# Threshold attention, then a gated MLP: the mask of chunk 0 of six early pairs moved from GpSimd to ScalarE (five) and VectorE (one)

## The chip, the cores and the metric

The kernel runs on one core of a Trainium2 chip. A core has a matrix engine (TensorE, PE in the profile), a vector engine (VectorE, DVE), an engine for functions of one value (ScalarE, ACT), a general engine (GpSimd, POOL), and SyncE (SP), which here only issues DMAs. They run side by side, each through its own list of instructions in order, and wait for one another with semaphores. The metric is the time of one execution on the device in microseconds (us), lower is better.

## The reference

The inputs are q, k and v of shape (8, 8, 576, 64): batch, heads, sequence, head size. All is float32.

```python
scores = scale * np.matmul(q, k.transpose(0, 1, 3, 2))          # scale = 1/8
thresh = np.max(scores, axis=-1, keepdims=True) - tau           # tau = 0.02
scores = np.where(scores >= thresh, scores, -1000000000.0)
scores = scores - np.max(scores, axis=-1, keepdims=True)
attn = np.exp(scores)
attn = attn / (np.sum(attn, axis=-1, keepdims=True) + 1e-09)
x = np.matmul(attn, v)                    # heads side by side: (8, 576, 512)

h = np.maximum(x @ w_in, 0.0)             # (8, 576, 1024)
u, v = h[..., :512], h[..., 512:]
v_n = (v - mean(v)) / np.sqrt(var(v) + 1e-06)
v_s = einsum('ts,bsd->btd', w_spatial, v_n) + b_spatial[None, :, None]
return (u * v_s) @ w_out                  # (8, 576, 512)
```

In the softmax, a score more than tau below the maximum of its row counts as zero. What is kept of a row before the division is called its numerators here. The division is done after the product with v, by a row sum that comes out of that product as a further column.

## The kernel before

**Pairs, chunks, steps.** Two heads form a pair; there are 32 pairs, four to a batch. The 576 queries of a pair are cut into chunks 0 to 3 of 128 and a rest of 64. The rests of an even pair and the next odd one are taken together as chunk 4 at the start of the odd pair. The list `steps` thus has 144 entries (i, c): four for an even pair, in the order 0, 1, 2, 3, and five for an odd one, in the order 4, 0, 1, 2, 3. Step numbers 0 to 3 are pair 0, 4 to 8 pair 1, 9 to 12 pair 2, 13 to 17 pair 3, and so on; pair 7 begins with step 31.

**One step.** `step(i, c, fs)` (line 599) writes out the order of every engine by hand:

- TensorE forms the scores of the chunk for both heads in a PSUM tile `s` (lines 562 and 567). There are two such tiles, so that the scores of a step are made while those of the step before are being read.
- Up to two small jobs of the list `fs` follow on TensorE, with their evictions: the transposes of the next pair's q and k (line 246), products with v (290, 295), and, from step 26 on, the matmuls of the gated MLP, one job a step.
- VectorE takes the negated maximum of each row, `negm` (line 611).
- ScalarE reads `s` twice, once per head, and writes `e` (float32, 128 x 1152, three buffers).

**The mask**, in three forms. For chunks 2 and 4 (`on_act`, line 571) VectorE first adds tau to the negated maximum (line 615). ScalarE then applies Prelu with a slope of 1e30 (line 628): where score - maximum + tau is negative, the result is hugely negative, elsewhere it is unchanged. A further Exp (line 630) turns that into the bf16 numerators, with zeros where the score was under the threshold; exp(tau) cancels in the division. For the other chunks ScalarE applies Exp directly (line 634), and one step later `mask()` (line 575) compares `e` with `ctau` = exp(-tau) and multiplies. For chunks 1 and 3, and for chunk 0 of pairs 0 and 7 to 31, that is one instruction of VectorE (line 592). For chunk 0 of pairs 1 to 6 it is two of GpSimd, which write a bf16 tile `keep` of ones and zeros (line 587) and then the product (line 589).

The numerators lie in `p` (four tiles, each with two chunks). After chunk 1 and after chunk 3, `mask()` has SyncE issue a DMA that transposes the whole tile to `pT` (line 596). For chunk 4 the numerators lie in `pr`. They are transposed on TensorE for the first six pairs (the three entries of `r_on_pe`), with an eviction at line 394, and by DMA after that. This is so before and after the change.

**What else the queues hold.** SyncE issues all loads of q, k and v for two pairs at a time, one DMA a step, into a ring of two slots, and these DMAs stand in one queue with the transposes. GpSimd, in order, copies the loaded q and k into the order that the transposes need (line 137, at chunk 2), casts v to bf16 (157, 161, at chunk 0), copies a small piece of k into `kd` (269), which the next pair's scores need, casts the weights in the first 55 steps (174, 203, 206, 182), and from step 26 on does the small arithmetic of the normalisation (453 to 465). ScalarE also evicts the transposes (251, 253, 264), those of x (375) and of `pr` (394), and the MLP's products (445, 459, 492, 541). VectorE also does the division (302, 304) and the gating (521, 524).

Of the kernel before, what the change touches and what calls it, by code (L numbers as in the profile page):

```python
# [9 lines left out]
BF16 = mybir.dt.bfloat16  # L10
AX = mybir.AxisListType
ALU = mybir.AluOpType
# [5 lines left out]
def kernel(  # L18
# [17 lines left out]
    nc = tc.nc  # L36
# [6 lines left out]
    P = 128  # L43
    const = ctx.enter_context(tc.tile_pool(name="const", bufs=1))
# [19 lines left out]
    ctau = const.tile([P, 1], F32, name="ctau")  # L64
# [25 lines left out]
        for t in vn_ring:  # L90
            nc.vector.memset(t[64:128, 4, :], 1.0)

    keep = const.tile([P, 1152], BF16, name="keep")
    w_in = const.tile([P, 4, 1024], BF16, name="w_in")
    w_o = const.tile([P, 4, 512], BF16, name="w_o")
    wsT = const.tile([P, 5, 640], BF16, name="wsT")
# [455 lines left out]
    def scores(i, c):  # L552

        s = ps_s.tile([P, 1536], F32, name="s")
        if c < 4:
            who = [(i, slice(c * P, (c + 1) * P), slice(0, P))]
        else:
            who = [(i - 1 + k, slice(512, 576), slice(64 * k, 64 * k + 64)) for k in range(2)]  # L560
        for n, m, rows in who:
            nc.tensor.matmul(out=view(s[rows], 512, [[448, 2], [1, 64]]), lhsT=qks[n][:, 0, m],  # L562
                             rhs=kd_ring[n % 2], start=True, stop=True)
        for h in range(2):
            hs = slice(64 * h, 64 * h + 64)
            for n, m, rows in who:
                nc.tensor.matmul(out=s[rows, 1024 * h:1024 * h + 512], lhsT=qks[n][hs, 0, m],  # L567
                                 rhs=qks[n][hs, 1, 0:512], start=True, stop=True)
        return view(s, 0, [[960, 2], [1, S]])

    def on_act(c):

        return c in (2, 4)

    def mask():
        i, c, e = unmasked.pop()
        if c == 4:
            dst = pts[i // 2] = ptr_ring[i // 2 % 2]
            if i // 2 in r_on_pe:
                return  # L580
            nc.sync.dma_start_transpose(out=dst, in_=pr_ring[i // 2 % 2])
            return
        pt = p_ring[2 * (i % 2) + c // 2]
        if c == 0 and 0 < i < 7:

            ef = e.rearrange("p h s -> p (h s)")
            nc.gpsimd.tensor_scalar(out=keep, in0=ef, scalar1=ctau, scalar2=1.0,  # L587
                                    op0=ALU.is_ge, op1=ALU.mult)
            nc.gpsimd.tensor_tensor(out=pt[:, c % 2, :], in0=ef, in1=keep, op=ALU.mult)  # L589
        elif not on_act(c):  # L590
            ef = e.rearrange("p h s -> p (h s)")
            nc.vector.scalar_tensor_tensor(out=pt[:, c % 2, :], in0=ef, scalar=ctau, in1=ef,  # L592
                                           op0=ALU.is_ge, op1=ALU.mult)
        if c % 2:
            dst = pts[i, c // 2] = ptp.tile([P, 2, 9, P], BF16, name="pT")
            nc.sync.dma_start_transpose(out=dst.rearrange("p c b s -> p (c b) s"),
                                        in_=pt.rearrange("p c s -> p (c s)"))

    def step(i, c, fs):

        s = scores(i, c)
        while held:
            held.pop(0)()


        for kind, mm, ev in fs[:2]:
            mm()
            if kind == "act":
                ev()
        nm = small.tile([P, 2], F32, name="negm")  # L610
        nc.vector.tensor_reduce(out=nm, in_=s, axis=AX.X, op=ALU.max, negate=True)  # L611

        by = scale if c == 4 else 1.0
        if on_act(c):
            nc.vector.tensor_scalar(out=nm, in0=nm, scalar1=by, scalar2=float(tau),  # L615
                                    op0=ALU.mult, op1=ALU.add)
        for kind, mm, ev in fs[:2]:
            if kind == "dve":
                ev()
        due = [f for n, f in later if n <= 0]  # L620
        later[:] = [(n - 1, f) for n, f in later if n > 0]
        for f in due:
            f()
        e = ep.tile([P, 2, S], F32, name="e")
        if on_act(c):

            for h in range(2):
                nc.scalar.activation(out=e[:, h, :], in_=s[:, h, :], func=ACT.Prelu,  # L628
                                     bias=nm[:, h:h + 1], scale=by, alpha=1e30)
            nc.scalar.activation(out=pr_ring[i // 2 % 2] if c == 4 else p_ring[2 * (i % 2) + c // 2][:, c % 2],  # L630
                                 in_=e.rearrange("p h s -> p (h s)"), func=ACT.Exp)
        else:
            for h in range(2):
                nc.scalar.activation(out=e[:, h, :], in_=s[:, h, :], func=ACT.Exp,  # L634
                                     bias=nm[:, h:h + 1])
        ready = sends[:]
        sends.clear()
        if unmasked:
            mask()
        for f in ready:  # L640
            f()
        unmasked.append((i, c, e))
        for kind, mm, ev in fs[2:]:
            mm()
            if kind == "dve":
                ev()
            else:
                held.append(ev)
# [150 lines left out]
    with tc.manual_schedule():  # L799
# [23 lines left out]
        for g, (i, c) in enumerate(steps):  # L823
            if c == 2 and i + 2 < NPAIR:
                shape_qk(i + 2)
            if c == 0:
                shape_v(i)
            if c == 0 and i % 2 and i + 3 < NPAIR or g == 0:
                for w in range(3):
                    queue.extend(load(i + (3 if g else 2), 2, w))  # L830
            if g in chores:
                chores[g][0](chores[g][1])
            fs, small_ones = [], []
            if i + 1 < NPAIR and c < 3:
                fs.append(qk_rem(i + 1) if c == 1 else qk_main(i + 1, c // 2))
            if i and c == (2 if i % 2 else 3):
                fs.append(pv(i - 1, 0))
            if i > 1 and c == 4:
                fs.append(pv(i - 2, 1))
            if i % 2 and c == 3:  # L840
                fs.append(pv(i - 1, 1))
            if i % 2 and i > 1 and c == 1:
                small_ones = [pv_rest(i // 2 - 1)]
                fs += small_ones
            fs += [f(*a) for f, *a in jobs.get(g, [])]
            fs.sort(key=lambda f: (f[0] == "dve", f in small_ones))
            sends += queue[:1 if g > 3 else 2]
            del queue[:1 if g > 3 else 2]
            step(i, c, fs)
# [8 lines left out]
        while held:  # L858
            held.pop(0)()
        mask()  # L860
        inner.close()
        wide.append(ctx.enter_context(tc.tile_pool(name="ps_t", bufs=6, space=PSUM,
# [49 lines left out]
```

## Time and profile before

| | us |
|---|---|
| median of 3 runs (lowest to highest) | 501.4 (501.18 to 501.8) |
| profiled execution, its own time | 501.18 |
| its span, first to last instruction | 499.4 |
| TensorE busy | 457.5 |
| VectorE busy | 420.2 |
| ScalarE busy | 385.5 |
| GpSimd busy | 263.1 |
| `keep`, line 587: 6 instructions, each | 4.176 |
| GpSimd's product, line 589: 6 instructions, mean | 2.752 |
| VectorE's mask, line 592: 90 instructions, mean | 1.481 |
| ScalarE's further Exp, line 630 to `p`: 32 instructions, mean | 1.163 |
| bias plus tau on VectorE, line 615: 48 instructions, mean | 0.453 |

A line of the trace gives the start and the duration in us, the engine, the line of the kernel (L587 is line 587), the operation and the tiles, written as output<-input. In brackets stands the time that the engine was idle before the instruction, and what ended that idle time. PE is the matmul, PEld the loading of its weights. Times in the text are from the start of the span. In the slices of the page one slice is 12.5 us and a digit is the busy share in tenths; PEclk is the clock that TensorE was granted, in tenths of its full clock.

### The profile page before, as it was taken

To read this page: it belongs to the slowest core of one execution; us is meant where nothing else is said; L and a number is where in the kernel's file an instruction comes from. 1 tells how busy PE (TensorE), PEld (TensorE's weight loads), DVE (VectorE), ACT (ScalarE), POOL (GpSimd) and SP (SyncE) were. 2 spreads that over 40 slices of the span, in tenths; PEclk is the share of its full clock that TensorE was granted. 3 is DMA by queue.
4 is the path that set the end of the run, shared out by engine and by line. 5 is a ranking of instruction groups with operands and counts; after the bars stand their busy time and mean duration, and the time that the engine had idled before them with its cause. 6 is when DMAs were issued, how large, how long until landed. Compare 5 with 4: busy or idle time off the path is not lost.

```text
span 499.4 us, 9898 instructions
## 1 busy us (share of the span) xinstructions
PE 457.5 (92%) x3646; PEld 243.9 (49%) x3691; DVE 420.2 (84%) x557; ACT 385.5 (77%) x672; POOL 263.1 (53%) x415
## 2 busy tenths in 40 slices
PE   7768787859989999999999999999999999999995
PEld 4334443435455455545454555545455555545542
DVE  5897898866988998799988998899898998899573
ACT  4847667767897979788887989787987889797351
POOL 3597585998462764357433753366424744253021
PEclk9887988997999999999999999999999999999998
DMA  7947868768698989997899989999999989867523
GB/s 241 235 95 178 190 138 193 162 145 165 146 178 211 194 178 220 200 205 167 176 199 216 177 198 210 198 184 180 180 203 218 178 182 214 158 108 131 145 82 109
DMA packets 227568, 88.49 MB, mean 177 GB/s; under 512 B 197056, under 2 KB 221760, under 8 KB 227520
## 3 DMA queue, kind: packets, MB, share of 16 engines
q1 hardware_dynamic: 226864, 86.98, 83.3%
q8 instruction: 29, 0.48, 0.4%
q0 software_dynamic: 160, 0.52, 0.3%
q10 hardware_dynamic: 496, 0.36, 0.2%
q14 instruction: 19, 0.16, 0.1%
HBM read 33.31 MB, written 9.44 MB: 86 GB/s over the span
## 4 chain that ended last, share of the span: by engine, by line
PE 52%; ACT 19%; DVE 16%; issue 5%; POOL 4%; DMA 2%; SPq 0%; POOLq 0%; ACTq 0%; DVEq 0%
PE s L567 16%; DVE negm L611 7%; ACT e L634 6%; PE s L562 5%; DVE p L592 5%; PE f L246 5%; PE f L295 4%; ACT e L628 4%; PE f L536 4%; PE f L477 3%; DVE negm L615 3%; PE f L507 2%; PE f L435 2%; PE f L290 2%; POOL keep L587 2%
## 5 line engine op out<-in xcount | busy, mean ns | idle before, releaser
L611 DVE TENSOR_REDUCE negm<-s 128x2 f32<-128x1152 f32 x144 | 194.8, 1353 | 40.5 <-PE s L567 40.0
L567 PE MATMUL s<-qkT 64*128 64x512 f32 (+1 forms) x640 | 168.1, 659 | 0.0
L634 ACT ACTIVATE e<-s,negm 128x576 f32<-128x576 f32 x192 | 131.7, 741 | 14.7 <-POOL p L589 5.0
L592 DVE SCALAR_TENSOR_TENSOR p<-e,ctau 128x1152 bf16<-128x1152 f32 x90 | 133.3, 1481 | 4.3 <-ACT e L634 4.2
L562 PE MATMUL s<-kd,qkT 128*128 128x128 f32 (+1 forms) x320 | 66.1, 311 | 23.4 <-ACT e L634 11.8
L628 ACT ACTIVATE e<-s,negm 128x576 f32<-128x576 f32 x96 | 65.8, 737 | 26.0 <-DVE negm L615 13.5
L269 POOL COPY kd<-qkT 64x64 f32<-64x64 f32 x62 | 28.0, 452 | 85.6 <-ACT qkT L264 83.8
L562 PEld LDWEIGHTS s<-kd,qkT 128*128 128x128 f32 (+1 forms) x320 | 45.6, 184 | 42.0 <-ACT e L634 21.0
L567 PEld LDWEIGHTS s<-qkT 64*128 64x128 f32 (+1 forms) x640 | 43.4, 180 | 19.0 <-issue 4.4
L453 POOL TENSOR_SCALAR nmean<-sm 128x1 f32<-128x1 f32 (+1 forms) x35 | 14.7, 419 | 67.8 <-ACT vrel L445 67.6
L137 POOL COPY qn<-ql 128x640 f32<-128x640 f32 x31 | 38.3, 1235 | 16.3 <-DVE negm L615 6.0
L295 PEld LDWEIGHTS <-pT 128*128 128x128 bf16 x1024 | 42.3, 98 | 7.6 <-issue 5.3
L295 PE MATMUL f<-v,pT 128*128 128x65 bf16 x992 | 45.4, 195 | 0.0
L630 ACT ACTIVATE p<-e 128x1152 bf16<-128x1152 f32 x32 | 37.2, 1163 | 1.0
L290 PE MATMUL f<-v,pT 128*128 128x130 bf16 x124 | 27.3, 220 | 4.8 <-ACT qkT L253 1.9
L253 ACT COPY qkT<-f 128x512 f32<-128x512 f32 x31 | 18.2, 586 | 17.1 <-PE f L246 16.9
L507 PE MATMUL f<-wsT,vn 128*128 128x512 bf16 x119 | 30.7, 379 | 0.3
L465 POOL TENSOR_SCALAR vn<-vrel,rs,nm 128x512 bf16<-128x512 f32 (+1 forms) x34 | 27.3, 803 | 3.7
L477 PE MATMUL f<-xT,w_in 128*128 128x512 bf16 x97 | 27.8, 381 | 1.6 <-DVE xn L304 0.8
L435 PE MATMUL f<-w_in,xT 128*128 128x512 bf16 x102 | 28.2, 388 | 0.4 <-issue 0.2
L304 DVE TENSOR_TENSOR xn<-f,r 128x256 bf16<-128x256 f32 x62 | 26.3, 425 | 2.2
L246 PEld LDWEIGHTS f<-identf,qn 128*128 128x128 f32 x124 | 14.2, 150 | 26.9 <-POOL v L161 8.3
(170 smaller groups left out, 699.0 us busy)
## 6 DMA issues: line engine op xcount, KB each, us to landing
vl<-in_v_dram SPq DMA_DIRECT2D x16, 512.0 KB, 4.6
ql<-in_q_dram SPq DMA_DIRECT2D x15, 512.0 KB, 4.6
kl<-in_k_dram SPq DMA_DIRECT2D x15, 512.0 KB, 4.6
out_dram<-o SPq DMA_DIRECT2D x20, 256.0 KB, 3.1
uT<-in_moe_w_in_dram SPq DMA_DIRECT2D x3, 512.0 KB, 6.4
uT<-in_moe_w_spatial_dram SPq DMA_DIRECT2D x2, 576.0 KB, 5.5
vl<-in_v_dram SPq DMA_DIRECT2D x16, 64.0 KB, 4.0
pT<-p SPq DMA_TRANSPOSE x64, 5.3
```

The costliest lines, as they stand in the source:

```text
L137: nc.gpsimd.tensor_copy(out=t, in_=ld_ring[i // 2 % 2][w][:, 2 * (i % 2):2 * (i % 2) + 2].rearrange("p h c d -> p c h d"))
L246: nc.tensor.transpose(out=t[:, c * P:(c + 1) * P], in_=nat[i][which][:, c, :], identity=identf)
L295: nc.tensor.matmul(out=t[:, at + 65 * h:at + 65 * h + 65], lhsT=pt[:, 5 * h + j, :], rhs=vt[:, 6 * h + j, :], start=False, stop=(h == 1 an ...
L435: nc.tensor.matmul(out=t, lhsT=xts[b][:, f, c * P:(c + 1) * P], rhs=w_in[:, f, 512:1024], start=(f == 0), stop=(f == 3))
L477: nc.tensor.matmul(out=t, lhsT=w_in[:, m, f * P:(f + 1) * P], rhs=xts[b][:, m, 0:512], start=(m == 0), stop=(m == 3))
L507: nc.tensor.matmul(out=t, lhsT=vn[:, c, f * P:(f + 1) * P], rhs=wsT[:, c, 0:512], start=(c == 0), stop=(c == 4))
L562: nc.tensor.matmul(out=view(s[rows], 512, [[448, 2], [1, 64]]), lhsT=qks[n][:, 0, m], rhs=kd_ring[n % 2], start=True, stop=True)
L567: nc.tensor.matmul(out=s[rows, 1024 * h:1024 * h + 512], lhsT=qks[n][hs, 0, m], rhs=qks[n][hs, 1, 0:512], start=True, stop=True)
L592: nc.vector.scalar_tensor_tensor(out=pt[:, c % 2, :], in0=ef, scalar=ctau, in1=ef, op0=ALU.is_ge, op1=ALU.mult)
L611: nc.vector.tensor_reduce(out=nm, in_=s, axis=AX.X, op=ALU.max, negate=True)
L628: nc.scalar.activation(out=e[:, h, :], in_=s[:, h, :], func=ACT.Prelu, bias=nm[:, h:h + 1], scale=by, alpha=1e30)
L634: nc.scalar.activation(out=e[:, h, :], in_=s[:, h, :], func=ACT.Exp, bias=nm[:, h:h + 1])
```

## The change

For chunk 0 of pairs 1 to 5, `on_act` now holds: VectorE adds tau to the negated maximum, ScalarE applies Prelu and then the further Exp into `p`, and `mask()` has nothing to do for that chunk. For chunk 0 of pair 6, `mask()` uses VectorE's one instruction, as it does for pairs 0 and 7 to 31. GpSimd's two instructions and the tile `keep` are gone. The lists of jobs, loads and steps are the same, and no DMA is added or removed.

```diff
-    keep = const.tile([P, 1152], BF16, name="keep")
...
-    def on_act(c):
-
-        return c in (2, 4)
+    def on_act(i, c):
+
+        return c in (2, 4) or c == 0 and 0 < i < 6
...
         pt = p_ring[2 * (i % 2) + c // 2]
-        if c == 0 and 0 < i < 7:
-
-            ef = e.rearrange("p h s -> p (h s)")
-            nc.gpsimd.tensor_scalar(out=keep, in0=ef, scalar1=ctau, scalar2=1.0,
-                                    op0=ALU.is_ge, op1=ALU.mult)
-            nc.gpsimd.tensor_tensor(out=pt[:, c % 2, :], in0=ef, in1=keep, op=ALU.mult)
-        elif not on_act(c):
+        if not on_act(i, c):
             ef = e.rearrange("p h s -> p (h s)")
             nc.vector.scalar_tensor_tensor(out=pt[:, c % 2, :], in0=ef, scalar=ctau, in1=ef,
                                            op0=ALU.is_ge, op1=ALU.mult)
...
-        if on_act(c):
+        if on_act(i, c):
             nc.vector.tensor_scalar(out=nm, in0=nm, scalar1=by, scalar2=float(tau),
                                     op0=ALU.mult, op1=ALU.add)
...
-        if on_act(c):
+        if on_act(i, c):
 
             for h in range(2):
                 nc.scalar.activation(out=e[:, h, :], in_=s[:, h, :], func=ACT.Prelu,
```

## The prediction

> **What bounds the kernel now.** I read the share of busy time by engine first, then the slices, to see where the kernel is not at its limit.
>
> ```profile
> PE 457.5 (92%) x3646; PEld 243.9 (49%) x3691; DVE 420.2 (84%) x557; ACT 385.5 (77%) x672; POOL 263.1 (53%) x415
> PE   7768787859989999999999999999999999999995
> POOL 3597585998462764357433753366424744253021
> PEclk9887988997999999999999999999999999999998
> ```
>
> TensorE (PE) is full from the tenth slice to the end; in the first nine, about 112 us, it is not, its granted clock is down, and POOL has its busiest slices. The busy times of two kinds of stretch say more. The first row is the stretch of the six masks that change; it runs from the maximum of pair 1 chunk 2 to that of pair 7 chunk 1, which is 26 steps. The other two hold 27 steps each, from one chunk 2 to the chunk 2 six pairs later.
>
> ```profile
> core 0: us, PE busy (x) PEld busy (x) DVE busy (x) ACT busy (x) POOL busy (x), PEclk, DMA share, GB/s
> 26.30:119.00 92.70, 72.81 (x545) 39.08 (x549) 74.65 (x78) 62.97 (x104) 74.08 (x76) 0.87 0.72 158
> 136.00:218.80 82.80, 79.77 (x664) 43.20 (x672) 73.01 (x94) 70.70 (x126) 42.40 (x75) 1.00 0.95 199
> 218.80:301.50 82.70, 80.76 (x665) 42.76 (x670) 75.59 (x97) 70.98 (x126) 45.80 (x79) 1.00 0.97 189
> ```
>
> The early stretch takes 92.7/26 = 3.57 us a step, the later ones 82.75/27 = 3.06, though these also hold the gMLP matmuls of every step, which the early one has only from step 26 (its last seven steps). So the early stretch does less and is slower, and no engine in it is full: TensorE 79%, VectorE (DVE) 81%, ScalarE (ACT) 68%, POOL 80%, DMA 72%. Something serialises them. The instructions around the first POOL mask, in order of time, show what (start, duration; in brackets the idle time before and its end):
>
> ```profile
> 27.52 4.18 POOL L587 TENSOR_SCALAR keep<-e,ctau 128x1152 bf16<-128x1152 f32 x1
> ...
> 27.70 4.01 DVE L615 TENSOR_SCALAR negm<-negm 128x2 f32<-128x2 f32 x1
> ...
> 31.78 2.37 POOL L589 TENSOR_TENSOR p<-e,keep 128x1152 bf16<-128x1152 f32 x1
> 31.81 1.37 ACT L628 ACTIVATE e<-s,negm 128x576 f32<-128x576 f32 x2 [4.34 <-DVE r L302]
> 32.12 3.24 DVE L592 SCALAR_TENSOR_TENSOR p<-e,ctau 128x1152 bf16<-128x1152 f32 x1
> ...
> 33.28 0.77 PE L562 MATMUL s<-kd,qkT 128*128 128x128 f32 x2 [3.21 <-issue]
> ```
>
> A DVE instruction on 128x2 elements, 0.17 us where nothing disturbs it, takes 4.01 us and ends with POOL's `keep` (27.52 + 4.18 = 31.70). Then the DVE mask, 1.41 us elsewhere, takes 3.24 while POOL's second instruction runs. ACT waits 4.34 us for the bias and TensorE 3.21 for ACT. The sixth mask costs in another way: POOL reaches it late, and ACT waits for the buffer `e` that POOL still reads.
>
> ```profile
> 103.62 4.18 POOL L587 TENSOR_SCALAR keep<-e,ctau 128x1152 bf16<-128x1152 f32 x1
> 107.88 2.36 POOL L589 TENSOR_TENSOR p<-e,keep 128x1152 bf16<-128x1152 f32 x1
> 110.27 1.37 ACT L634 ACTIVATE e<-s,negm 128x576 f32<-128x576 f32 x2 [3.84 <-POOL p L589]
> 111.69 0.80 PE L562 MATMUL s<-kd,qkT 128*128 128x128 f32 x2 [4.56 <-ACT e L634]
> ```
>
> **The change part by part.** The sum is against the profiled execution: span 499.4, its own time 501.18, the lowest of the three runs (median 501.4).
>
> *Taken away: six pairs of POOL instructions.* 6 x 4.18 + 16.5 (L589 together) = 41.6 us of POOL. POOL's own time is worth nothing; what it held up is. (a) DVE L615, five times under `keep`: 4.01 + 1.42 + 2.00 + 2.00 + 2.00, less 5 x 0.17 = 10.6 us. Two more (0.67 and 0.87, under POOL copies that came late) give 1.2. (b) DVE L592 under L589, twice: 2 x (3.24 - 1.41) = 3.7. (c) ACT waiting for POOL to release `e`: 5.0 in three waits, the longest 3.84. (d) After three of these stalls TensorE's scores ran at a lower clock: one group's four 64x512 products took 2.08 us and its two remainder products 0.77 to 0.80, against 1.13 and 0.46 at the full clock: 3 x 1.3 = 3.9. Together 24.4 us, nearly all of it on the chain of waits.
>
> *Added on ACT.* Chunk 0 of pairs 1 to 5 takes the form of chunk 2. Prelu in place of Exp from the scores costs the same (737 ns at L628, 741 at L634, twice a step either way). The further Exp to bf16 costs 1.163 us, five times: 5.8 us. Queued behind it on ACT are the evictions of the next step and chunk 1's two activations, for which TensorE waits (s has two buffers). ACT had been waiting in these steps, so part of the 5.8 falls into room; ACT goes from 62.97 to 68.8 us in the stretch and becomes its busiest engine, 2.65 us a step. That is the load of the later stretches (70.8/27 = 2.62).
>
> A rule speaks against this part: the Trainium skill, ScalarE: Activation LUTs, Rules for kernel authors, budgets about 2.7 us for every switch to another set of functions; were Prelu and Exp in different sets, ten switches would add 27 us and the change would lose. The trace has chunks 2 and 4 alternating them 48 times with one table load, 1.28 us, before the first step; so I take nothing for it.
>
> *Added on DVE.* Five more L615 at 0.17 = 0.9 us, and the mask of pair 6 chunk 0 at 1.41. DVE without the stalls has 74.65 - 11.8 - 4.3 (L592, with 0.6 at 111.68) = 58.6, and so 60.9 afterwards, 2.34 a step against 2.75 later. Each L615 is now in front of ACT's Prelu; it can be held by POOL's other instructions, since chunk 0 is also where POOL casts v. The 37 L615 after 120 us exceed 0.17 by 1.83 us together, 0.05 each: 0.25 us. Lower end nothing, upper end 5 x 0.72 (a whole v cast, L157) = 3.6; I take 0.3, as the later steps have the same casts.
>
> The Trainium skill, SBUF — State Buffer, Who interferes with whom, says that the shared port is held for a GpSimd instruction's whole length; it would put every meeting at the full 0.72, and the sum 3.3 us worse. The rows say the meetings are rare.
>
> *Queues.* No DMA is added or removed. SP's transposes of `p` for chunks 0 and 1 wait, as before, for chunk 1's DVE mask (26.0 us of SP's waits before 130 us), and the loads behind them on SP come earlier with it. On POOL, what stood behind the masks (q, k and v copies, `kd`, weight casts) comes up to 6.9 us earlier; the loads that overwrite the same ring then go out earlier too. Dropping `keep` frees memory and no time.
>
> *What is late next.* Removed 24.4, added 5.8 + 2.3 + 0.3: 16.0 if the additions all lie on the path. As a check by floors: at the later pace, 3.06 a step, the 26 steps take 79.7, a gain of 13.0; no engine would then carry more than about 1% above its later load per step (ACT 2.65 against 2.62, DMA 0.72 x 92.7/26 = 2.57 against 2.94, TensorE at most 2.80 against 2.97). With ACT 95% busy, 68.8/0.95 = 72.4, a gain of 20.3; with DMA 95% busy, 66.7/0.95 = 70.2, a gain of 22.5. Between 13.0 and 20.3 the middle is 16.7. I take 17: 501.2 - 17 = 484.2, and 484.5 for the median. The later steps move forward unchanged: TensorE is 97% busy there.
>
> **The rivals.**
>
> *ACT sets the pace, and less is gained.* For it: the later 85% of ACT give 68.8/0.855 = 80.5, a gain of 12.2; with the 3.6 us of held L615 8.6, so 489 to 493. Against it: ACT's 85% there lie beside a TensorE at 97%, which has room in the early stretch.
>
> *DMA or ACT is packed to its floor, and more is gained.* A gain of 20.3 to 24.4 gives 477 to 481. For it: the two catch-up steps from 65.15 took 1.8 and 2.65 us. Against it: every stall left the DMA time to run ahead, which it loses.
>
> *The later steps pay it back: slower.* The DMA is 95 to 97% busy there, and 17 us less go before it. If the prefetch then runs dry, each of the 24 pairs after pair 7 waits for its transposed `p` or its loads; the point from which this decides is 17/24 = 0.71 us a pair, and at 1 us a pair the time is 508. Against it: TensorE's L290 waited for `pT` 4.1 us in the whole span, and the steps' pace has been that of TensorE for 300 us, long past any start.
>
> *The stall stays.* If something else held DVE, only the 5.0 us (c) would go, against 5.8 + 2.3 added: 501 to 505. Against it: all five long L615 end within 0.03 us of the end of a `keep`, and the longest after 125 us is 0.59.
>
> **How the numbers follow.** Forecast 0.70 (479 to 489), ACT's pace 0.13, packed further 0.10, paid back or stall kept 0.05, no difference 0.02. The spread of the three runs is 0.12%, so 0.2%, about 1 us, tells a change from none. The range 478 to 493 leaves out the two last cases and the ends of the second and third. Faster 0.93, same 0.02, slower 0.05.
>
> **What would show it.** No L615 above about 1 us before 130 us, L592 near 1.41 throughout; the early 26 steps in 72 to 80 us with ACT near 69 busy, a granted clock above 0.95 and POOL near 33 busy; the wait of ACT for POOL gone; the last of the waits in that stretch TensorE's for ACT. Wrong would be: a `s` wait of TensorE for ACT of about 1.2 us in each chunk 0, L615 held by v casts, DMA at 95% in the early stretch with POOL waiting for loads, or the later stretches above 82.8 us.

## The result

The changed kernel takes 479.75 us (median of four runs, 478.85 to 480.29) against 501.29 us before (four runs, 499.13 to 501.8). The ratio is 0.9576, with a 95% interval of 0.9544 to 0.9608: faster by 21.5 us, where 17 were forecast. The time lies in the range given, 478 to 493, near its lower end.

Line numbers are those of the changed kernel in this section: L604 is the maximum (L611 before), L608 the addition of tau (L615), L585 VectorE's mask (L592), L621 Prelu (L628), L623 the further Exp (L630), L627 Exp (L634). The lines of the page that answer to those of before:

```profile
PE 447.0 (94%) x3646; PEld 239.6 (50%) x3691; DVE 410.2 (86%) x563; ACT 389.9 (82%) x677; POOL 225.9 (47%) x403
PE   7788888889999999999999999999999999999995
POOL 3553344895448543574417642565336744252021
PEclk9999999999999999999999999999999999999999
```

TensorE does the same work in 10.5 us less of busy time, as its granted clock no longer falls in the stretch: no slice is under 0.9, and the mean of the execution is 1.00 where it was 0.97. The stretch of the six masks, again from step 7 to step 33, and a later stretch (busy times of the engines, clock, DMA share, GB/s):

```profile
core 0: us, PE busy (x) PEld busy (x) DVE busy (x) ACT busy (x) POOL busy (x), PEclk, DMA share, GB/s
26.40:97.00 70.60, 62.89 (x545) 34.65 (x549) 62.92 (x82) 65.77 (x107) 34.83 (x59) 1.00 0.96 203
115.30:198.00 82.70, 79.75 (x664) 43.14 (x672) 73.91 (x95) 70.18 (x125) 42.26 (x74) 1.00 0.93 197
```

Step 7 starts its maximum at 26.39 us (26.31 before) and step 33 at 97.01 (118.96 before). So the 26 steps fell from 92.65 to 70.62 us, by 22.0. What follows step 33 takes 380.7 us, against 380.4: the gain was made in that one stretch, and nothing was given back. ScalarE is now 93% busy there, VectorE 89%.

The same place in the work as in the lines shown of before, pair 1 from its chunk 2 on:

```profile
27.42 0.49 PE L561 MATMUL s<-kd,qkT 128*128 128x128 f32 x2
27.79 0.26 DVE L608 TENSOR_SCALAR negm<-negm 128x2 f32<-128x2 f32 x1
...
28.08 1.37 ACT L621 ACTIVATE e<-s,negm 128x576 f32<-128x576 f32 x2 [0.23 <-DVE negm L608]
...
28.50 1.42 DVE L585 SCALAR_TENSOR_TENSOR p<-e,ctau 128x1152 bf16<-128x1152 f32 x1
...
30.27 0.46 PE L561 MATMUL s<-kd,qkT 128*128 128x128 f32 x2
```

The addition takes 0.26 us instead of 4.01, the mask 1.42 instead of 3.24. ScalarE waits 0.23 us instead of 4.34, and TensorE starts the next scores at 30.27 instead of 33.28, at the full clock (0.46 instead of 0.77).

The waits between the engines in the stretch (in total, times, longest), the main ones of before:

```profile
ACT e L628 <- DVE r L302: 9.1, 4, 4.3
PE s L562 <- ACT e L634: 8.1, 8, 4.6
ACT e L634 <- POOL p L589: 5.0, 3, 3.8
```

The first names the reciprocal that stands right behind the addition of tau; what ScalarE needs is the addition's result. What is left between TensorE, VectorE and ScalarE:

```profile
DVE negm L604 <- PE s L566: 7.3, 9, 1.8
PEld s L561 <- ACT e L627: 5.1, 9, 0.9
PE s L561 <- ACT e L627: 3.6, 7, 0.8
ACT e L627 <- DVE negm L604: 1.9, 3, 0.9
```

ScalarE's waits for GpSimd are gone, and the longest wait of a matmul for ScalarE's Exp is 0.8 us, where it had been 4.56 at the sixth mask.

### The profile page after: what moved, and what is told of

Its sections match the earlier page's. It is cut to its first block, busy times and chain, and to the rows that moved or that the text cites. A ratio compares the mean times of both kernels' runs of the same rounds, so it can differ in the third digit from the quotient of the medians.

```text
span 477.7 us, 9895 instructions
## 1 busy us (share of the span) xinstructions
PE 447.0 (94%) x3646; PEld 239.6 (50%) x3691; DVE 410.2 (86%) x563; ACT 389.9 (82%) x677; POOL 225.9 (47%) x403
## 4 chain that ended last, share of the span: by engine, by line
PE 49%; ACT 22%; DVE 20%; issue 6%; DMA 2%; POOL 0%; POOLq 0%; DVEq 0%; ACTq 0%
PE s L566 14%; DVE negm L604 10%; DVE p L585 7%; ACT e L621 6%; ACT e L627 5%; PE f L294 4%; PE f L245 4%; PE s L561 4%; PE f L535 4%; PE f L476 3%; ACT sq L458 2%; ACT vrel L444 2%; ACT p L623 2%; PE f L506 2%; PE f L289 2%
## 5 line engine op out<-in xcount | busy, mean ns | idle before, releaser
L604 DVE TENSOR_REDUCE negm<-s 128x2 f32<-128x1152 f32 x144 | 194.8, 1353 | 32.2 <-PE s L566 31.8
L566 PE MATMUL s<-qkT 64*128 64x512 f32 (+1 forms) x640 | 161.9, 636 | 0.0
L585 DVE SCALAR_TENSOR_TENSOR p<-e,ctau 128x1152 bf16<-128x1152 f32 x91 | 133.5, 1468 | 1.2 <-ACT e L627 1.2
L627 ACT ACTIVATE e<-s,negm 128x576 f32<-128x576 f32 x182 | 124.9, 741 | 6.2 <-DVE negm L604 6.0
L621 ACT ACTIVATE e<-s,negm 128x576 f32<-128x576 f32 x106 | 73.0, 743 | 14.4 <-DVE negm L608 9.3
L561 PE MATMUL s<-kd,qkT 128*128 128x128 f32 (+1 forms) x320 | 64.5, 304 | 12.1 <-ACT e L627 6.6
L561 PEld LDWEIGHTS s<-kd,qkT 128*128 128x128 f32 (+1 forms) x320 | 44.2, 179 | 30.9 <-ACT e L627 15.7
L566 PEld LDWEIGHTS s<-qkT 64*128 64x128 f32 (+1 forms) x640 | 41.9, 174 | 18.2 <-issue 2.7
L452 POOL TENSOR_SCALAR nmean<-sm 128x1 f32<-128x1 f32 (+1 forms) x35 | 15.7, 449 | 68.4 <-ACT vrel L444 61.5
L623 ACT ACTIVATE p<-e 128x1152 bf16<-128x1152 f32 x37 | 43.0, 1163 | 1.2
L136 POOL COPY qn<-ql 128x640 f32<-128x640 f32 x31 | 33.5, 1081 | 16.4 <-DMA ql<-in_k_dram 11.5
L464 POOL TENSOR_SCALAR vn<-vrel,rs,nm 128x512 bf16<-128x512 f32 (+1 forms) x34 | 29.9, 880 | 3.7
L444 ACT ACTIVATE vrel<-f 128x512 f32<-128x512 f32 (+1 forms) x34 | 20.1, 592 | 7.4 <-PE f L260 3.0
```

What stands on the lines that cost most here:

```text
L136: nc.gpsimd.tensor_copy(out=t, in_=ld_ring[i // 2 % 2][w][:, 2 * (i % 2):2 * (i % 2) + 2].rearrange("p h c d -> p c h d"))
```

## The experiments

Each was timed beside the kernel before on the same chip; the chips differ by up to 2 us, so the length of the stretch from step 7 to step 33 in the profile (92.65 before, 70.62 changed) is given too. A theory and two rivals stood at the start. The theory: a GpSimd instruction that reads SBUF keeps VectorE out, and that was the cost. One rival: the cost was GpSimd's lateness, through the buffer `e` and the copies queued behind the masks. The other: the changed kernel has come to a floor of ScalarE or of the DMA, which hides what the parts are worth. Of each edit the lines that matter are shown; the tiles that it needs besides (`keep`, `wide_src`, `ptau`, `spare`) are declared and filled in lines left out here.

### All six masks on VectorE

```diff
-        return c in (2, 4) or c == 0 and 0 < i < 6
+        return c in (2, 4)
```

> All six masks of chunk 0 as one VectorE instruction, none on GpSimd, none on ScalarE. Theory (what costs is a GpSimd instruction that reads SBUF beside VectorE, not where the mask goes): nearly the whole gain, 480 to 485; VectorE carries 5 x (1.41 - 0.17) = 6.2 us more than in the changed kernel. Rival (the changed kernel is at ScalarE's pace in the early steps): ScalarE loses 5.8 us, so below 477.

Measured: 480.98 us, ratio 0.9608 (0.9569 to 0.9646), the stretch 71.81. Nearly the whole gain is there without the further Exps on ScalarE, as the theory has it: leaving GpSimd is what counts. In this stretch VectorE is 95% busy (68.52 of 71.80 us) and ScalarE 85%, the changed kernel's picture turned round.

### The two parts alone

Pair 6 left on GpSimd, and then pair 6 alone taken off it. The first edit is to the changed kernel, the second to the kernel before:

```diff
-        if not on_act(i, c):
+        if c == 0 and i == 6:
+            ef = e.rearrange("p h s -> p (h s)")
+            nc.gpsimd.tensor_scalar(out=keep, in0=ef, scalar1=ctau, scalar2=1.0,
+                                    op0=ALU.is_ge, op1=ALU.mult)
+            nc.gpsimd.tensor_tensor(out=pt[:, c % 2, :], in0=ef, in1=keep, op=ALU.mult)
+        elif not on_act(i, c):
```

```diff
-        if c == 0 and 0 < i < 7:
+        if c == 0 and 0 < i < 6:
```

> Pairs 1 to 5 on ScalarE as changed, pair 6 left on GpSimd. Theory: the gain less the sixth mask's own stall (3.84 us of ScalarE's wait, 1.3 of the lower clock after it): 483 to 487. Rival (the sixth stall was only the lateness that the first five handed on to GpSimd): no more than 1 us above the changed kernel, 480 to 481.

> Only the mask of pair 6 moved to VectorE, pairs 1 to 5 left on GpSimd. Theory: a gain of 4 to 6 us, 495 to 497. Rival (lateness handed on): 498 to 501, as GpSimd is still late when pair 6 comes.

Measured: 485.74 us (ratio 0.9691, 0.9659 to 0.9722) and 495.21 us (0.9876, 0.9838 to 0.9915); the stretch 76.43 and 86.89. Both are as the theory has them. The sixth mask costs 76.43 - 70.62 = 5.8 us of the stretch with the other five gone and 92.65 - 86.89 = 5.8 with them in place. So its stall was its own, and not lateness handed on; the parts add up.

### The addition of tau taken off VectorE, the masks left on GpSimd

To the kernel before, for pairs 1 to 6:

```diff
-        if on_act(c):
+        if on_act(c) and not 0 < i < 7:
             nc.vector.tensor_scalar(out=nm, in0=nm, scalar1=by, scalar2=float(tau),
                                     op0=ALU.mult, op1=ALU.add)
...
         if on_act(c):
+            if 0 < i < 7:
+                nc.scalar.activation(out=nm, in_=nm, func=ACT.Identity, bias=ptau, scale=by)
```

> The kernel before, with the addition of tau for chunks 2 and 4 of pairs 1 to 6 on ScalarE instead of VectorE; all six masks stay on GpSimd. Theory (GpSimd's read keeps VectorE out): the 11.8 us of the long small instructions go, but VectorE's mask, next in its queue with two SBUF inputs, is held in their place until GpSimd's first instruction ends, so it shows 3 us and more; net gain 2 to 8 us, 493 to 499. Rival (VectorE waited for data, and its long duration is only how that is recorded): 500 to 503, with ScalarE's addition waiting as long instead.

Measured: 495.58 us, ratio 0.9886 (0.9845 to 0.9928), the stretch 85.81. The lines of this kernel in order of time (its L588 and L590 are GpSimd's two instructions, L593 is VectorE's mask):

```profile
25.42 4.18 POOL L588 TENSOR_SCALAR keep<-e,ctau 128x1152 bf16<-128x1152 f32 x1
...
27.46 0.29 ACT L628 ACTIVATE negm<-negm,ptau 128x2 f32<-128x2 f32 x1 [0.23 <-DVE negm L612]
...
27.89 2.57 DVE L593 SCALAR_TENSOR_TENSOR p<-e,ctau 128x1152 bf16<-128x1152 f32 x1
...
29.69 3.00 POOL L590 TENSOR_TENSOR p<-e,keep 128x1152 bf16<-128x1152 f32 x1
...
32.72 1.37 ACT L636 ACTIVATE e<-s,negm 128x576 f32<-128x576 f32 x2 [2.36 <-POOL p L590]
```

ScalarE does the same addition of 128x2 at once, in 0.29 us, in the middle of `keep`. So its data were there, and VectorE had not been waiting for data. VectorE's next instruction with SBUF inputs is now the one that is held: the mask starts at 27.89 and ends 0.86 us after `keep`, 2.57 us in all. The instruction between them, a product out of PSUM, ran at its usual 0.42 us beside `keep`. At the five places the masks now take 2.18 to 3.12 us, only one of them the 3 us and more that were expected.

The larger part of the wait moved to where the expectation did not look. GpSimd's two instructions still read `e`, and ScalarE now waits for it after each of the six masks, as in the last line shown: 13.0 us in six waits, against 5.0 in three before. So the holding of `e` is a cost of its own, and in the kernel before it stood mostly behind VectorE's wait. With VectorE's additions out of GpSimd's way the stretch is still 85.81 - 70.62 = 15.2 us longer than in the changed kernel.

### A GpSimd instruction that reads, and one that only writes

To the changed kernel, at the place of the six old masks: once the comparison of a constant tile, once memsets of about the same time. Neither touches data of the kernel.

```diff
+        if c == 0 and 0 < i < 7:
+            nc.gpsimd.tensor_scalar(out=keep, in0=wide_src, scalar1=ctau, scalar2=1.0,
+                                    op0=ALU.is_ge, op1=ALU.mult)
```

```diff
+        if c == 0 and 0 < i < 7:
+            for _ in range(4):
+                nc.gpsimd.memset(keep, 1.0)
```

> The changed kernel plus, at the place of the old masks (chunk 0 of pairs 1 to 6), one GpSimd comparison of a constant 128 x 1152 float32 tile into a tile that nothing reads: 4.18 us of GpSimd each, no data of the kernel touched, no buffer held. Theory (a GpSimd instruction that reads SBUF keeps VectorE out): VectorE's small additions or masks show 2 to 4 us again beside it, 486 to 494. Rival (the old masks cost by holding e and by what waited for their result): no long VectorE instruction, at most 481.

> The changed kernel plus, at the same six places, four GpSimd memsets of 128 x 1152 bf16, some 4.5 us together: GpSimd is as occupied as in the run with the read, but only writes. Theory (reading matters): the masks of VectorE stay at 1.41 us, a small addition is held by one memset at most (1.1 us); 480 to 484. Rival (GpSimd's occupation, which makes its copies late, is the cost): as slow as the run with the read.

Measured: 495.91 us with the read (ratio 0.9913, 0.9882 to 0.9945; stretch 85.81) and 481.23 with the writes (0.9619, 0.9592 to 0.9646; stretch 71.99). The read is 2 us above the range expected of it. From the trace with the read (L613 is the addition of tau, L590 VectorE's mask):

```profile
57.62 4.17 POOL L586 TENSOR_SCALAR keep<-wide_src,ctau 128x1152 bf16<-128x1152 f32 x1
...
58.63 3.19 DVE L613 TENSOR_SCALAR negm<-negm 128x2 f32<-128x2 f32 x1
...
61.85 1.37 ACT L626 ACTIVATE e<-s,negm 128x576 f32<-128x576 f32 x2 [3.17 <-DVE r L303]
```

and from the trace with the writes (L612 is the addition, L589 the mask):

```profile
37.22 4.40 POOL L586 MEMSET keep<- 128x1152 bf16 x4
38.27 1.15 DVE L612 TENSOR_SCALAR negm<-negm 128x2 f32<-128x2 f32 x1
38.37 1.42 DVE L589 SCALAR_TENSOR_TENSOR p<-e,ctau 128x1152 bf16<-128x1152 f32 x1
```

Six reads of a constant, which hold no buffer and for which nothing waits, bring back 15.2 of the 22.0 us. Five of VectorE's additions are long again (2.63, 3.20 and three of 3.19, together 14.5 us over their usual 0.17), and they end with `keep`: 58.63 + 3.19 = 61.82 here, 57.62 + 4.17 = 61.79. With the writes GpSimd is as occupied (53.1 us busy in the stretch, 54.9 with the read), its copies are as late, and the stretch is 1.4 us longer than in the changed kernel: four additions wait for one memset each (1.10 to 1.15 us), and the masks in this stretch stay between 1.40 and 1.47. So the lateness of GpSimd's copies is not the cost. That VectorE is kept out is.

That it takes a reading instruction is shown for the mask: 1.42 us beside a memset, 2.57 beside `keep` in the run with the addition on ScalarE, 3.24 beside GpSimd's product in the kernel before. It is not shown for the addition, which the memset holds too, until it ends. One memset takes 1.06 us and the read 4.17, so for the additions the two runs differ in the length of GpSimd's instruction as well as in what it does, and no run with one long write tells the two apart.

The Trainium skill, SBUF — State Buffer, Who interferes with whom, says that a VectorE instruction in a two-port mode contends with GpSimd, and that one with two SBUF inputs contends with a GpSimd instruction that reads SBUF and not with one that only writes it. The masks, which have two SBUF inputs, agree with it by the numbers above; that the addition runs in a two-port mode no run shows.

### More work for ScalarE, and for the DMA

To the changed kernel: the further Exp of chunk 0 of pairs 1 to 5 done twice, and, in another kernel, one further load of 512 KB in each of these pairs.

```diff
+            if c == 0:
+                nc.scalar.activation(out=keep, in_=e.rearrange("p h s -> p (h s)"), func=ACT.Exp)
```

```diff
+            if 0 < i < 6 and c == 1:
+                sends.append(lambda: nc.sync.dma_start(
+                    out=spare, in_=q[7, 0:4, 0:512, :].rearrange(
+                        "h (p c) d -> p h (c d)", c=4)))
```

> The changed kernel with ScalarE's further Exp of chunk 0 of pairs 1 to 5 done twice (the second into a tile that nothing reads): 5 x 1.163 = 5.8 us more on ScalarE. Theory as on record (part of it lies on the path): 2 to 5 us slower, 481.5 to 484.5. Rival A (ScalarE has room for it): within 1 us, at most 480.7. Rival B (ScalarE sets the pace already): the whole 5.8, 485 and more.

> The changed kernel plus one load of 512 KB from HBM in chunk 1 of each of pairs 1 to 5, into a tile that nothing reads; 5 x 512 KB at the early stretch's 203 GB/s are 13 us of the DMA engines. If the DMA is the floor of the early stretch (96% busy): 488 to 493. If its share only looks full: at most 483.

Measured: 483.97 us with the Exp twice (ratio 0.9686, 0.9657 to 0.9715; stretch 76.38) and 479.83 with the loads (0.9603, 0.9575 to 0.963; stretch 70.60). The busy times of the two stretches, the Exp first:

```profile
26.30:102.70 76.40, 65.20 (x548) 35.33 (x549) 63.77 (x82) 70.86 (x113) 35.34 (x61) 0.98 0.90 186
```

```profile
27.20:97.80 70.60, 63.10 (x548) 34.63 (x549) 62.68 (x82) 65.79 (x107) 34.15 (x61) 1.00 1.03 232
```

With the Exps done twice the stretch is 76.38 - 70.62 = 5.8 us longer. ScalarE is busy 5.1 us longer in it (70.86 against 65.77; the second Exp of pair 1 starts just ahead of it), so the added work costs all of its time and a little more; the granted clock is 0.98 here, and TensorE is busy 2.3 us longer for the same work. ScalarE had no room left. The time, 483.97 us, lies in the range of the theory on record and not in that of rival B; as a ratio it is 4.2 to 5.5 us above the changed kernel (0.9686 against 0.9603 and 0.9576), which does not tell the two apart. The loads cost nothing: 2.6 MB more were loaded, the rate rose from 203 to 232 GB/s, and the steps kept their pace. A DMA share of 0.96 in the changed kernel is not a floor.

### The removal alone, and two other ways to share the masks

In chunk 0 of pairs 1 to 6, no mask at all; then the masks shared, odd pairs on ScalarE and even ones on VectorE; then pair 6 on ScalarE too; and the changed kernel again, beside them.

```diff
-        return c in (2, 4) or c == 0 and 0 < i < 6
+        return c in (2, 4)
...
-        if not on_act(i, c):
+        if not on_act(i, c) and not (c == 0 and 0 < i < 7):
...
+                to = (p_ring[2 * (i % 2)][:, 0, h * S:(h + 1) * S] if c == 0 and 0 < i < 7
+                      else e[:, h, :])
-                nc.scalar.activation(out=e[:, h, :], in_=s[:, h, :], func=ACT.Exp,
+                nc.scalar.activation(out=to, in_=s[:, h, :], func=ACT.Exp,
```

```diff
-        return c in (2, 4) or c == 0 and 0 < i < 6
+        return c in (2, 4) or c == 0 and i in (1, 3, 5)
```

```diff
-        return c in (2, 4) or c == 0 and 0 < i < 6
+        return c in (2, 4) or c == 0 and 0 < i < 7
```

> Chunk 0 of pairs 1 to 6 without a threshold: ScalarE's Exp writes the bf16 numerators directly, no mask on any engine. The threshold of those six chunks is left out, so this is the price of the removal alone. Theory as on record (24.4 us removed, the added 8.5 on the path): 8.5 us below the changed kernel. What the run with the Exp done twice suggests (each us of ScalarE in the early steps counts in full, and the removal was worth more than 24.4): 5 to 8 us below. If the early steps are at a floor that is not ScalarE's or VectorE's: within 2 us of it.

> The masks shared out: pairs 1, 3 and 5 on ScalarE, pairs 2, 4 and 6 on VectorE. ScalarE has 2.3 us less than in the changed kernel, VectorE 2.5 more. If ScalarE alone sets the early pace: 1.5 to 2.5 us faster than the changed kernel. If the two engines set it together: within 1 us.

> The mask of pair 6 on ScalarE too: 1.16 us more there, 1.24 less on VectorE. If each us of ScalarE counts in full: 1 us slower than the changed kernel. Else: the same.

> The changed kernel once more, on the same chip as the other three, as their measure: a ratio of 0.957 plus or minus 0.004 to the kernel before.

| | us | ratio to before | stretch |
|---|---|---|---|
| changed kernel again | 480.03 | 0.9603 (0.9568 to 0.9637) | 70.60 |
| no mask in the six chunks | 478.99 | 0.9581 (0.9552 to 0.961) | 69.36 |
| odd on ScalarE, even on VectorE | 480.34 | 0.9606 (0.958 to 0.9632) | 70.24 |
| pair 6 on ScalarE too | 481.47 | 0.9638 (0.9602 to 0.9675) | 72.35 |

The changed kernel again is within the 0.957 plus or minus 0.004 expected. Without any mask the stretch is only 1.2 us shorter than there. So the removal alone is worth 92.65 - 69.36 = 23.3 us, and all that the change added costs 1.2. Neither the 8.5 us of the theory on record nor the 5 to 8 that the doubled Exp suggested came; within 2 us was the third case. Sharing the masks out gives 0.4 us of the stretch and nothing in the time, where ScalarE as the only limit would have given 1.5 to 2.5. The sixth mask on ScalarE costs 1.75 us of the stretch for 1.16 of ScalarE's work, with overlapping intervals in the time. No run was clearly faster than the changed kernel with the whole computation done.

```profile
26.30:95.70 69.40, 62.76 (x549) 34.55 (x547) 60.45 (x77) 61.84 (x103) 30.96 (x60) 1.00 0.94 204
```

That is the stretch without any mask. TensorE is at 90%, ScalarE at 89%, VectorE at 87%, and the DMA was shown to have room. More work on ScalarE made these steps longer, less of it (61.84 us here, 65.77 in the changed kernel) made them hardly shorter, so ScalarE alone is not what holds them. The round from the scores to the maximum to ScalarE and back through the two buffers `s` would do it, but no run with a third buffer was made, and this stays open.

## Why the prediction was right, and where its size was off

**The mechanism** was right. VectorE was kept out by GpSimd's instructions: in the five places the long addition is gone, and six reads of a constant brought it back, with 15.2 us. What the prediction had too small is the second cost beside it, (c), ACT waiting for POOL to release `e`. Its rows showed 5.0 us; with the addition done on ScalarE they show 13.0. The two overlap: six reads that hold no buffer cost 15.2 us, and with VectorE's additions out of the way, but `e` and the masks held, 15.2 of the 22.0 remain as well. Leaving GpSimd takes away both.

**"Together 24.4 us"**, what is removed: 23.3 by the run without a mask. That the total comes so near is in part luck, as the terms are not what they were taken for: (c) and the clock are larger, and all of them overlap. Only at pair 6 can (c) and the clock after it be read alone: 5.8 us, against the 3.84 + 1.3 of the rows.

**"Added 5.8 + 2.3 + 0.3: 16.0 if the additions all lie on the path"** is the step that was mis-sized. They cost 1.2. I saw that ACT had been waiting in these steps and that part of the 5.8 would fall into room, but took the room for small, because ScalarE's load of 2.65 us a step is that of the later steps. It was the wrong comparison: in the later steps ScalarE's 85% stands beside a TensorE that is 97% busy, and need not be a limit of its own. The room was about as large as what the change put into it. The same five Exps once more cost 5.8.

**The floors.** The 17 were taken near the middle between the later pace (a gain of 13.0) and ScalarE at 95% (20.3). The stretch came out at 70.6 us, below ScalarE's 72.4, as ScalarE had 65.8 us in it and not 68.8. One of the five further Exps, that of pair 1, runs at 24.78 us, ahead of the stretch, so only four were to be added there. The durations of ScalarE's instructions in it do add up to 4.7 us more (75.1 against 70.4), but instructions that follow one another closely overlap in the records, and busy time counts an overlap once: it rose by 2.8. At 70.6 the stretch is also below the 72 to 80 us named as a sign of being right. 93% busy is close to what was taken for the floor. The DMA's 70.2 us is the nearest number, and by coincidence: the loads showed that 2.6 MB more do not move it. The time lies in the forecast's 479 to 489 and also in the 477 to 481 of the rival in which DMA or ACT is packed to its floor, which I gave 0.10; the gain of 21.5 is nearer to that rival than to the 17. Its reason is not shown: the DMA took 2.6 MB more, and without any mask ScalarE has 3.9 us less to do and the stretch is only 1.2 us shorter.

**The clock.** I counted 3.9 us for three stalls. TensorE's busy time in the stretch fell from 72.8 to 62.9 us for the same instructions, so 9.9 us of slow clock were there. In the profile before, the granted clock is 0.50 in four places of the stretch, from 32.7 to 42.9, 63.4 to 66.8, 77.1 to 80.4 and 111.2 to 118.0 us; (d) counted three, and one group of scores in each. How much of the 9.9 lay beside other waits no run shows.

**VectorE's remaining meetings with GpSimd.** The additions were put at 0.3 us together; in the stretch the four longest are 0.33 and three of 0.26, so 0.4 over their usual time. The 3.6 us for five whole casts, the upper end, was far too much. What I did not price are the masks: three of them take 1.83, 1.72 and 2.34 us beside GpSimd's copies and casts, 1.7 us over their usual 1.41, so "L592 near 1.41 throughout" did not hold.

**The functions.** The changed kernel has one table load, as before, so no switch was paid. The load took 1.28 us; by that, ten switches would have been an estimated 12.8 us, not 27.

**The rivals of the other sign** did not come. What follows step 33 takes 380.7 us against 380.4, so nothing was paid back.

## What to carry to other kernels

Before work is given to an idle GpSimd, look at what VectorE runs beside it: one reading GpSimd instruction of 4.18 us made a VectorE instruction of 0.17 us last 4.01, and ScalarE waited 4.34 us for it and TensorE 3.21. The sign of it in a trace is a tiny VectorE instruction that ends with a GpSimd one. Look too at which buffer GpSimd holds while it reads: when the first wait was taken away here, ScalarE waited 13.0 us for `e`. And an addition to an engine with waits in it is not priced by its busy share elsewhere: five further Exps on ScalarE cost at most 1.2 us of the stretch, the same five again 5.8, so measure where the room ends.

## What was not expected of the hardware

A share of 0.96 to 1.03 of DMA busy time was no limit: 2.6 MB more of loads raised the rate from 203 to 232 GB/s and left the 26 steps at 70.6 us. And GpSimd's occupation as such cost little: 53 us busy with memsets of 1.06 us each in the stretch made it 1.4 us longer, 55 us with six reads of 4.17 us in their place 15.2.
